# From attention to mixing: where the raw mixing weights land, and the order of the last output tiles

## The chip, the core and the metric

The kernel runs on one core of a Trainium2 chip. A core has five engines that work at the same time, each through its own queue and in program order: TensorE (PE in the profile; PEld is its weight load), VectorE (DVE), ScalarE (ACT), GpSimd (POOL) and SyncE (SP). In this kernel SP issues every DMA. An engine that waits for another one stands still with everything queued behind it. The metric is the device time of one execution in microseconds (us).

## What is computed

One block with an adaptive layer norm: attention over a sliding window of 256 keys with 32 heads, then a block that mixes neighbouring rows, then an MLP. The sequence has 2048 rows of 576 numbers, all in float32.

```python
mod = (_silu(c) @ w_mod).reshape(c.shape[0], 6, 1, -1)
sa, ca, ga, sb, cb, gb = (mod[:, i] for i in range(6))
h = _layernorm(x) * (1 + ca) + sa
x = x + ga * attention(h, wqkv, wo)          # 32 heads of 18, window 256
h = _layernorm(x) * (1 + cb) + sb
# the second block, on h:
g = _gelu(_layernorm(h) @ w1)                # four quarters of the columns,
hs = shift(g) @ w2                           # shifted by +1, -1, +2, -2 rows
x1 = h + hs
b = x1 + _gelu(_layernorm(x1) @ w3) @ w4
out = x + gb * b
```

## The kernel before

The rows are cut into 16 tiles of 128 (`t`, 0 to 15) and these into eight groups of two for the mixing. A float32 product is made of three: each operand is split into a high part (a cast to the matmul's format) and a low part (the rest), and high by high, high by low and low by high are added up. So each weight passes through ACT (the cast) and DVE or POOL (the subtraction), and each activation that PE transposed goes through ACT and DVE before the next product can use it.

Every piece of work is a small function that `at(time, function, ...)` puts into one list with a time of its own; `build` sorts the list by these times and calls the functions in that order (L1242). The times are no more than an order: they decide in which sequence each engine and SP meet their instructions. `te` is the time at which attention's two pools of buffers are closed, `T1` the time of the first mixing product, `tm(h)` the time of head h, 13 units each.

Around the change stand three streams of work.

*The end of attention.* A quad of heads u (0 to 15; four heads on two packed pairs) ends with `av` (L512, product of the exponentials P and the values V, on PE), `avs` (L529, ACT copies it from PSUM), `otr` (L533, PE transposes), `onm` (L538, DVE divides by the row sums) and `ost` (L546, SP stores it to DRAM). The last of them is u = 15.

*The output tiles.* `wotile` (L645) is the chain for one tile of rows: `orow` (SP loads the attention's rows and x), `otT` (PE transposes), `otev` (ACT and DVE split), `wom` (PE, two halves of 14 products with Wo), `woe` (DVE adds x), `ln1`, `ln1n`, `ln2`, `ln2n` (the two layer norms, on DVE, POOL and ACT) and the stores `st1`, `st2`, `st3` to three arrays in DRAM: `xp` (the residual), `hbd` (h) and `xnd` (normed h). Tiles 0 to 9 run beside the attention; tiles 10 to 15 come after `av` of u = 15, since a tile from 12 on needs its store, or stand close to it.

*The mixing.* `begin` (L706) opens the pools `mixb` and `mixa`. `w1load` and `w2load` bring the raw weights in five pieces each, `w1split` and `w2split` split them. Per group, `load` brings two rows of `xnd`, `tr` transposes, `tev` splits, `w1mm` makes five products, `w1ev` the GELU and its split, `w2mm` the second product of a tile in two halves, `w2ev` adds h (loaded by `hload`), and `st`, `nrm`, `rsum`, `xst`, `rst` make the norm and the residual for the MLP (`xpl` loads the residual; `gb` is the factor that it is scaled with, loaded at L873).

Memory sets a second order. A pool gives out buffers by tag: x1, rr, xm are three, three and two buffers of 576 floats for the mixing's residual, gf two of 256 floats for the GELU; the tag xr of `mixa` has three buffers of 640 floats, and before the change all raw W1, raw W2 and loaded rows go through these three in turn. The pools of attention and of mixing lie on the same (left) side, one over the other in time: a tile that lies over an older one waits until that one's last reader is done, tile by tile. From the bottom, attention has the four Q tiles, the three K tiles, the QS tiles, the maxima, then V, KS and P.

## Time and profile before

| | |
|---|---|
| median of 3 runs | 1869.98 us (1864.36 to 1878.24) |
| the profiled execution | 1870.27 us, span 1868.5 us |
| mean granted clock of PE | 0.971 |
| PE busy | 1731.3 us, 93% |
| DVE / POOL / ACT busy | 1094.4 / 902.3 / 707.2 us |
| DMA, mean over the span | 111 GB/s |

The page gives busy times of the engines over the span; the timeline lists instructions of an engine in order of time (start, length, engine, line, operation, tiles, count, and in brackets the idle time before it with what ended it). The windows view cuts the span into stretches: for each, its length, the busy time of PE, PEld, DVE, ACT and POOL, then the clock that was granted to PE (1.00 is full), the share of the DMA engines in use and GB/s. The waits view says who waited for whom: us in total, times, longest. Line numbers are those of the kernel before.

The change lies between 700 us and 830 us of the span: attention's last `av` starts at 719.17 us, group 0's first mixing product (L789) at 746.87 us, and group 1's at 783.30 us. From 971 us on the MLP's products (L1128 and others) fill the rest.

### The profile page before, as it was taken

The numbers are of one execution on the slowest core, as the hardware profiler recorded it, in microseconds if no ns is written. First come the engines' busy times: TensorE is split into PE (matmuls) and PEld (weight loads), VectorE is DVE, ScalarE is ACT, GpSimd is POOL, SyncE is SP. The second block draws the span as 40 slices with busy tenths as digits, with TensorE's granted clock in tenths as the row PEclk, the third lists the DMA queues.
The fourth block names the chain that finished last, engine by engine and source line by source line (L and its number), as shares of the span: only waits on it lengthen the run. The fifth ranks groups of instructions, "written<-read, shape, count | busy, mean of one in ns | idle before, by whom it ended". The sixth has DMA issues, their size and how long they took to land.

```text
span 1868.5 us, 33751 instructions
## 1 busy us (share of the span) xinstructions
PE 1731.3 (93%) x13496; PEld 1579.5 (85%) x13496; DVE 1094.4 (59%) x1801; ACT 707.2 (38%) x1210; POOL 902.3 (48%) x842
## 2 busy tenths in 40 slices
PE   6999989889999997898879999999979999999998
PEld 6788878788888986797868899999978999999997
DVE  3644244455656563566667666666676666666664
ACT  2222134344444444444433333333343333333331
POOL 3312264445454442346466655555553555555560
PEclk9999979899999998899989999999989999999999
DMA  4855552444544533565352211111224222222211
GB/s 146 312 180 180 165 152 85 118 117 133 156 134 141 149 101 113 192 216 168 115 167 68 60 55 54 55 55 56 60 71 141 60 60 60 60 60 60 59 43 51
DMA packets 156132, 206.72 MB, mean 111 GB/s; under 512 B 19012, under 2 KB 87620, under 8 KB 155400
## 3 DMA queue, kind: packets, MB, share of 16 engines
q1 hardware_dynamic: 155976, 204.57, 35.8%
q8 instruction: 106, 1.74, 0.4%
q14 instruction: 50, 0.41, 0.1%
HBM read 143.69 MB, written 60.56 MB: 109 GB/s over the span
## 4 chain that ended last, share of the span: by engine, by line
PE 45%; DVE 3%; POOL 3%; DMA 2%; ACT 1%; issue 1%; SPq 1%; POOLq 0%; DVEq 0%
PE d L1128 23%; PE pg L789 1%; PE w L838 1%; DVE W L986 1%; DMA wf<-in_B_w_dram 1%; PE u18P L1075 1%; PE u19P L1075 1%; PE u29P L1075 1%; PE u33P L1075 1%; PE u32P L1075 1%; PE u31P L1075 1%; PE u30P L1075 1%; PE u28P L1075 1%; PE u27P L1075 1%; PE u26P L1075 1%
## 5 line engine op out<-in xcount | busy, mean ns | idle before, releaser
L1128 PE MATMUL d<-W,G 128*128 128x288 f32 x3456 | 505.9, 297 | 11.9 <-DVE acc L1136 9.1
L1128 PEld LDWEIGHTS d<-W,G 128*128 128x128 f32 x3456 | 487.9, 189 | 33.6 <-DVE acc L1136 10.3
L1136 DVE TENSOR_TENSOR acc<-d,acc 128x576 f32<-128x576 f32 x288 | 216.7, 753 | 195.9 <-PE d L1128 193.9
L966 POOL TENSOR_TENSOR wf<-wf 128x384 f32<-128x384 f32 x140 | 146.6, 1068 | 337.9 <-DMA wf<-in_B_w_dram 299.8
L456 DVE TENSOR_REDUCE m<-mx 128x2 f32<-128x640 f32 x224 | 181.3, 817 | 159.5 <-PE mx L446 157.3
L504 ACT ACTIVATE P<-X 128x512 f32<-128x512 f32 (+4 forms) x320 | 180.4, 573 | 207.2 <-PE X L489 204.6
L444 PE MATMUL mx<-KD,QS 128*128 128x320 f32 (+4 forms) x512 | 157.6, 358 | 38.2 <-POOL QS L427 19.4
L427 POOL TENSOR_SCALAR QS<-QD,rowm 128x512 fp32r<-128x512 f32 x128 | 87.7, 698 | 145.4 <-DMA QD<-qd 60.7
L487 PE MATMUL X<-QD,KS 128*128 128x64 f32 (+2 forms) x704 | 151.2, 307 | 3.7 <-ACT P L504 3.3
L978 POOL TENSOR_TENSOR W<-wf,W 128x768 fp32r<-128x768 f32 x70 | 151.4, 2185 | 1.2 <-ACT W L972 1.2
L1105 DVE TENSOR_TENSOR G<-U,G 128x512 fp32r<-128x512 f32 x108 | 91.0, 843 | 100.3 <-ACT G L1098 100.3
L444 PEld LDWEIGHTS mx<-KD,QS 128*128 128x128 f32 x512 | 101.9, 199 | 45.8 <-POOL QS L427 24.2
L1096 ACT ACTIVATE U<-U 128x512 f32<-128x512 f32 x108 | 68.3, 632 | 177.6 <-DVE U L1081 177.6
L1096 ACT ACTIVATE C<-C 128x512 f32<-128x512 f32 x36 | 22.8, 632 | 280.7 <-DVE C L1081 280.7
L279 PE MATMUL qk<-hT,Wqk 128*128 128x512 f32 x504 | 121.0, 401 | 0.0
L279 PEld LDWEIGHTS qk<-hT,Wqk 128*128 128x128 f32 x504 | 95.9, 191 | 24.2 <-issue 0.9
L487 PEld LDWEIGHTS X<-QD,KS 128*128 128x128 f32 x704 | 106.7, 195 | 10.6 <-ACT P L504 7.5
L434 POOL TENSOR_SCALAR KS<-KD,rowm 128x768 fp32r<-128x768 f32 (+1 forms) x128 | 107.6, 853 | 0.0
L992 POOL TENSOR_TENSOR wf<-wf,gb 128x1152 f32<-128x1152 f32 x35 | 103.5, 2956 | 6.7 <-DMA wf<-in_B_w_dram 6.7
L446 PE MATMUL mx<-Mq,identr 128*128 128x128 f32 x448 | 101.3, 226 | 0.0
L1007 POOL TENSOR_TENSOR W<-wf,W 128x1152 fp32r<-128x1152 f32 x35 | 96.7, 2762 | 6.9 <-ACT W L1001 6.9
L972 ACT CAST W<-wf 128x1152 fp32r<-128x1152 f32 x70 | 90.3, 1319 | 21.6 <-DMA wf<-in_B_w_dram 10.8
(763 smaller groups left out, 3219.5 us busy)
## 6 DMA issues: line engine op xcount, KB each, us to landing
wf<-in_B_w_dram SPq DMA_DIRECT2D x35, 576.0 KB
wf<-in_B_w_dram SPq DMA_DIRECT2D x140, 128.0 KB
KD<-kd SPq DMA_DIRECT2D x72, 216.0 KB
QD<-qd SPq DMA_DIRECT2D x96, 144.0 KB
wf<-in_B_w_dram SPq DMA_DIRECT2D x140, 64.0 KB
qd<-qs SPq DMA_DIRECT2D x16, 512.0 KB
kd<-qs SPq DMA_DIRECT2D x16, 512.0 KB
vd<-Vst SPq DMA_DIRECT2D x16, 312.0 KB
```

Source lines behind the costliest of these rows:

```text
L279: nc.tensor.matmul(po, W[:, a, fs], H[:, c, :], start=(n == 0), stop=(n == 13))
L434: nc.gpsimd.tensor_scalar(t[:, b0:, r], src[:, b0:], M[:, 2 + r:3 + r], 0.0, op0=ALU.mult, op1=ALU.add)
L444: nc.tensor.matmul(pm[:, s, 320 - 64 * nb:320], lhs, K[:, j, 64 * (i + 5 - nb):64 * (i + 5)], start=True, stop=False)
L456: nc.vector.tensor_reduce(out=m[:, c:c + 2], in_=pm[:, :, 0:320], axis=mybir.AxisListType.X, op=ALU.max, negate=True)
L487: nc.tensor.matmul(px[:, c:c + q1 - q0], K[:, b + 4].rearrange("p r k -> p (r k)"), Q[:, j, q0:q1], start=(i == 0), stop=False)
L504: nc.scalar.activation(p[:, lo:], X["px", n, j, k][:, lo:], AF.Exp, scale=SCALE)
L966: nc.gpsimd.tensor_tensor(out=WF[:, o], in0=WF[:, a], in1=WF[:, b], op=ALU.subtract)
L978: eng.tensor_tensor(out=W[:, s0:s1, 3:5, :], in0=WF[:, 1 + s0:1 + s1, 0:2], in1=W[:, s0:s1, 0:2, :].bitcast(F32), op=ALU.subtract)
L992: nc.gpsimd.tensor_tensor(out=R4, in0=R4, in1=gb.unsqueeze(1).to_broadcast([P, 2, D]), op=ALU.mult)
L1075: nc.tensor.matmul(po, W[:, w - 1, a, :], X[:, b, :], start=(m == 0), stop=(m == 6))
L1128: nc.tensor.matmul(po, G[:, g, ta, b, ts], W[:, w, b, cs], start=(n == 0), stop=(n == 5))
L1136: nc.vector.tensor_tensor(out=a, in0=po, in1=a, op=ALU.add)
```

## The change

Six things are done at once.

- Raw W1 (five pieces), the first two row tiles of the mixing and the first piece of raw W2 get buffers of the tags x1, rr, xm and gf in `mixb`, which are asked for first in `begin` and so lie at the bottom of the left side; raw W2's last piece takes a buffer of x1. Only raw W2's pieces 1 to 3 and the rows from tile 2 on use the tag xr of `mixa`.
- Raw W1, the two row tiles and four pieces of raw W2 are loaded at `te` + 0.1 to 0.3 in place of `te` + 0.1 to 0.5 (W1), 8 and 9 (rows) and 17 to 23 (W2). The 64 last columns of the first two rows go to a buffer of their own, by two DMAs each in place of one.
- W1 is split from `te` + 0.6 on and not from 7.5, ahead of `avs` of u = 15 and of tile 10's `otT`; W2 from 8.5 and not from 19.
- The first two rows are transposed at `te` + 5.7 and 6.8, ahead of tile 10's products, and not at 15 and 16, behind tile 11's.
- `T1` is `te` + 14.3 and not `te` + 19: the mixing as a whole moves up by 4.7 units.
- The chain of u = 15 and tiles 10 to 15 are written out with times of their own (`last`). Relative to the mixing, tile 11's products stand between group 0's first products, tile 12's at their end, tiles 13 and 14 in group 1 and tile 15 in group 2. The store of u = 15 and the load of tile 12's rows stand at 13.3 and 13.4 (9.5 and 9.75 before). The load of `gb` moves from 15 to 24.

```diff
@@ attention
         for u in range(16):
             h = 2 * u + LX + 2
             at(tm(h), av, u)
+            if u == 15:
+                continue
...
+        def last(te):
+            for r in range(2):
+                at(te + 5.0 + .01 * r, avs, 15, r)
+                at(te + 9.9 + .1 * r, otr, 15, r)
+                at(te + 11.4 + .1 * r, onm, 15, r)
+            at(te + 13.3, ost, 15)
+            for t, b0, o, a, w0, w1 in ((10, 0, -8.0, 5.02, 7.9, 11.6), (11, 2, .05, 13.6, 15.95, 17.65), (12, 2, 13.4, 19.75, 21.15, 23.2),
+                                        (13, 2, 21.2, 32.1, 33.75, 35.45), (14, 2, 29.2, 37.55, 38.9, 40.6), (15, 2, 42.5, 49.85, 51.5, 53.2)):
+                at(te + o, orow, t)
+                at(te + a, otT, t, b0)
+                at(te + a + .02, otev, t)
+                for hf, w in ((0, w0), (1, w1)):
+                    at(te + w, wom, t, hf, b0)
+                    at(te + w + 2.05, woe, t, hf)
+                e = te + w1 + 2.1
+                for d, f in ((.3, ln1), (1.0, st1), (3.0, ln1n), (4.9, ln2), (5.5, st2), (7.5, ln2n), (9.5, st3)):
+                    at(e + d, f, t)
@@ mixing, begin
+            for t in range(2):
+                X["xr", t] = mb([P, D], F32, tag="x1", name=f"xmr{t}", bufs=3)
+                X["xt", t] = mb([P, 256], F32, tag="gf", name=f"xmt{t}", bufs=2)[:, 0:P]
+            X["w1", 0] = mb([P, D], F32, tag="x1", name="w1r0", bufs=3)
             X["W2"] = mb([P, 9, D], F32R, name="W2")
+            for k in range(1, 5):
+                X["w1", k] = mb([P, D], F32, tag="rr" if k < 4 else "xm", name=f"w1r{k}", bufs=3 if k < 4 else 2)
+            X["w2", 0] = mb([P, D], F32, tag="xm", name="w2r0", bufs=2)
...
@@ mixing, load
+            if t > 1:
+                X["xr", t] = ma([P, 640], F32, tag="xr", name=f"xmr{t}", bufs=3)
+                X["xt", t] = X["xr", t][:, 512:]
+            r = X["xr", t]
             nc.sync.dma_start(r[:, 0:D], self.xnd[t])
-            nc.sync.dma_start(r[:, D:], self.xnd[t][:, 512:])
+            if t > 1:
+                nc.sync.dma_start(r[:, D:], self.xnd[t][:, 512:])
+            else:
+                for u in range(2):
+                    nc.sync.dma_start(X["xt", t][:, u * TAIL:(u + 1) * TAIL], self.xnd[t][:, 512:])
@@ mixing, times
-            at(T0 + .1 + .1 * k, w1load, k)
-            at(T0 + 7.5 + 1.5 * k, w1split, k)
-            at(T0 + 17 + 2 * k, w2load, k)
-            at(T0 + 19 + 2 * k, w2split, k)
-        at(T0 + 15, lambda: nc.sync.dma_start(self.gb, self.modd[5].to_broadcast([P, D])))
+            at(T0 + .1 + .01 * k, w1load, k)
+            at(T0 + .6 + .8 * k, w1split, k)
+            at(T0 + (.2 + .01 * k if k < KC else 7.0), w2load, k)
+            at(T0 + (8.5, 11, 14.5, 17.7, 22)[k], w2split, k)
+        at(T0 + 24, lambda: nc.sync.dma_start(self.gb, self.modd[5].to_broadcast([P, D])))
@@ mix_events
-            at(s - 7, load, t)
+            at(s - 7 if t > 1 else T1 - 14.14 + .01 * t, load, t)
...
-            tile_in(i, T1 - 4 + i)
+            tile_in(i, T1 - 8.6 + 1.1 * i)
@@ build
-            T1 = te + 19.0
-            wotile(10, 33.95, 0)
-            wotile(11, 34.5, 0)
-            wotile(12, 35.22)
-            for i, d in enumerate((6.7, 18.2, 35.9)):
-                wotile(13 + i, (T1 + d - tm(0)) / HU - 0.3)
+            T1 = te + 14.3
+            last(te)
```

More of the change, by code (lines that the diff above doesn't have):

```diff
@@ L693, in attention @@
             wotile(t, 12.4 + 2 * t)
-        return tm, wotile
+        def last(te):
[15 more added lines that the diff above has]
+                    at(e + d, f, t)
+        return tm, last
     def mixing(self, T0, TB):
@@ L718, in w1load @@
         def w1load(k):
-            r = X["w1", k] = ma([P, 640], F32, tag="xr", name=f"w1r{k}", bufs=3)
+            r = X["w1", k]
             if k < KC:
@@ L740, in w2load @@
         def w2load(k):
-            r = X["w2", k] = ma([P, 640], F32, tag="xr", name=f"w2r{k}", bufs=3)
+            if k == KC:
+                X["w2", k] = mb([P, D], F32, tag="x1", name=f"w2r{k}", bufs=3)
+            elif k:
+                X["w2", k] = ma([P, 640], F32, tag="xr", name=f"w2r{k}", bufs=3)
+            r = X["w2", k]
             if k < KC:
@@ L759, in load @@
         def load(t):
-            r = X["xr", t] = ma([P, 640], F32, tag="xr", name=f"xmr{t}", bufs=3)
+            if t > 1:
+                X["xr", t] = ma([P, 640], F32, tag="xr", name=f"xmr{t}", bufs=3)
+                X["xt", t] = X["xr", t][:, 512:]
+            r = X["xr", t]
             nc.sync.dma_start(r[:, 0:D], self.xnd[t])
-            nc.sync.dma_start(r[:, D:], self.xnd[t][:, 512:])
+            if t > 1:
[3 more added lines that the diff above has]
+                    nc.sync.dma_start(X["xt", t][:, u * TAIL:(u + 1) * TAIL], self.xnd[t][:, 512:])
         def tr(t):
@@ L768, in tr @@
                 nc.tensor.transpose(pt[:, 0, k * P:(k + 1) * P], r[:, k * P:(k + 1) * P], self.ident)
-            nc.tensor.transpose(pt[:, 1, 0:P], r[:, 512:], self.ident)
+            nc.tensor.transpose(pt[:, 1, 0:P], X["xt", t], self.ident)
         def tev(t):
@@ L1224, in build @@
             t1, t2 = self.qkv(0.0, 47.0)
-            tm, wotile = self.attention(t1, t2, t1 + 6.0, HU)
+            tm, last = self.attention(t1, t2, t1 + 6.0, HU)
             te = tm(34.07)
```

## The prediction

> **What bounds the kernel now.** I read the page first: TensorE (PE) is busy 93% of the span and every other engine 59% or less, so an edit pays only where PE stands still or runs at a lower granted clock. The forecast is made against the profiled execution: 1868.5 us of span, 1870.27 us as a run, 0.3 us above the median of 1869.98 us.
>
> ```profile
> span 1868.5 us, 33751 instructions
> ...
> PE 1731.3 (93%) x13496; PEld 1579.5 (85%) x13496; DVE 1094.4 (59%) x1801; ACT 707.2 (38%) x1210; POOL 902.3 (48%) x842
> ```
>
> Next I read the timeline of PE around the place that the diff touches, from the last attention product, u = 15 at L526 (it ends at 719.17 + 4.86 = 724.03; I call this moment A), to the first product of mixing group 1 at L789 (783.30).
>
> ```profile
> 719.17 4.86 PE L526 MATMUL av<-P,V 64*32 64x320 f32 x208
> 723.96 0.66 PE L590 MATMUL pa<-ident,or 128*128 128x128 f32 x4
> ...
> 726.01 2.13 PE L611 MATMUL wo<-Wo,T 128*128 128x288 f32 x14 [1.29 <-DVE T L599]
> 727.99 1.03 PE L536 MATMUL ot<-ident,avs 128*128 128x128 f32 x8
> 728.78 2.09 PE L611 MATMUL wo<-Wo,T 128*128 128x288 f32 x14
> ...
> 740.67 0.66 PE L768 MATMUL ptm<-ident,xmr 128*128 128x128 f32 x4 [3.81 <-DMA xmr<-xnd]
> ...
> 745.89 1.12 PE L590 MATMUL pa<-ident,or 128*128 128x128 f32 x4 [2.78 <-DMA or<-od]
> ...
> 777.39 6.07 PE L838 MATMUL w<-W,Gm 128*128 128x288 f32 x28 [5.82 <-DVE xr L615]
> 783.30 1.82 PE L789 MATMUL pg<-xT,W 128*128 128x256 f32 x14
> 784.97 0.60 PE L590 MATMUL pa<-ident,or 128*128 128x128 f32 x4
> ```
>
> Brackets hold PE's idle time and what ended it: the first rows' load, the output rows' load (it follows the store of u = 15), and a long wait before the first W2 product. Then the windows view, for this stretch, the next one, and the parts at half clock (the sum line covers 741.19 to 751.43, 758.25 to 761.67 and 775.32 to 782.15).
>
> ```profile
> 724.03:783.30 59.27, 41.27 (x258) 38.77 (x259) 31.20 (x69) 21.30 (x49) 19.28 (x30) 0.83 0.60 187
> 783.30:832.47 49.17, 47.65 (x382) 47.29 (x380) 33.02 (x84) 23.57 (x54) 22.18 (x37) 1.00 0.59 197
> ...
> sum 20.49, PE 15.40 PEld 14.68 DVE 14.27 ACT 5.73 POOL 6.37; mean PE 5.13 PEld 4.89 DVE 4.76 ACT 1.91 POOL 2.12
> ```
>
> The second figure is PE's busy time: idle is 59.27 - 41.27 = 18.0 us. PE worked 15.40 us at a granted clock of 0.50, half of which, 7.7 us, a full clock would save. So the stretch loses 25.7 us, and no reordering in it can gain more. The next 49 us hold 1.5 us of idle. What is won must be won before 783.30.
>
> **Why the clock fell.** Cut into pieces of 3.41 us from a fall at 707.06, the windows view shows the fall follow an idle piece:
>
> ```profile
> 724.12:727.54 3.42, 2.13 (x16) 1.89 (x16) 0.89 (x2) 1.74 (x4) 0.00 (x0) 1.00 0.65 187
> 727.54:730.95 3.41, 3.41 (x28) 3.22 (x27) 2.26 (x7) 1.54 (x4) 1.85 (x3) 1.00 0.76 257
> ...
> 737.78:741.19 3.41, 0.52 (x5) 0.52 (x5) 0.47 (x1) 0.00 (x0) 2.15 (x3) 1.00 0.69 199
> 741.19:744.60 3.41, 1.68 (x8) 0.93 (x6) 1.92 (x5) 1.51 (x4) 0.00 (x0) 0.50 0.45 119
> ...
> 748.02:751.43 3.41, 3.41 (x18) 3.41 (x17) 0.53 (x2) 0.00 (x0) 0.14 (x1) 0.50 0.90 277
> 751.43:754.84 3.41, 2.90 (x23) 2.66 (x21) 0.00 (x0) 1.23 (x2) 0.50 (x1) 1.00 0.97 317
> ```
>
> A piece with 0.52 us of PE work is followed by half clock; one with 2.13 us is not; a full piece (3.41 us) brings full clock back.
>
> **The change part by part.**
>
> *Loads ahead of A.* SP, the queue that issues all DMAs, stands idle before A; it waited 12.6 us for the last attention product ahead of the first raw W1:
>
> ```profile
> SPq L721 <- PE av L526: 12.6, 1, 12.6
> ...
> 711.01 0.45 SPq L584 DMA_DIRECT2D xr<-in_A_x_dram  x1
> 724.12 2.05 SPq L721 DMA_DIRECT2D w1r<-in_B_w_dram  x3
> ...
> 739.46 0.43 SPq L548 DMA_DIRECT2D od<-o  x1
> 742.92 0.32 SPq L581 DMA_DIRECT2D or<-od  x1
> ```
>
> The raw W1 buffers lie over P tiles, which u = 15 reads. Now raw W1, the two first rows and the first raw W2 go to the residual's tags x1, rr, xm, gf, which open at the bottom of the same side; by the tiles' sizes (x1, gf: 8,960 bytes; W2; rr, xm: to 41,216) they lie over Q0 to Q2, K2 and QS, whose last readers are the products of heads 30 and the maxima of heads 31. So SP goes on at 711.5: row loads of tile 11 (3 DMAs), W1 (6), first rows (6, two more than before, as the 64-wide tail is now loaded twice), one W2: 16 issues. At 2.05 / 3 = 0.68 us each that is at most 10.9 us: 722.4. All of it lies beside u = 15, so it costs nothing; were the cover gone it would be 11 us of SP time ahead of everything after A (second rival). Raw W2 1 to 3 keep the old buffers: SP waits there until A, and behind it stand raw W2 4 (8 DMAs), the store of u = 15 and tile 12's rows. The store's data come only with onm, at about 735.5; the rows are issued 742.92 - 739.46 = 3.5 us later and land 745.89 - 742.92 = 3.0 us after that, near 742; PE asks for them near 747.5. Hidden, with 5 us to spare. The zero fill of gk on POOL now lies over a V tile and waits for A; only W1's POOL subtractions are queued behind it, and they are needed 11 us later. The late load of gb needs no cover until the first rsum, ten us behind it. None of this is on the path.
>
> *The order at A on ACT.* Here the change adds a wait. W1 itself still lies over V tiles that u = 15 reads, so its casts can start between 719.3 (if nothing held them) and 724.1 (A); V is read to the end but for the last blocks of keys, so I take 723.4. They stand ahead of avs and of tile 10's otev in ACT's queue, where before otev came first (724.65).
>
> ```profile
> 724.65 0.58 ACT L597 CAST T<-pa 128x512 fp32r<-128x512 f32 x1 [4.78 <-PE pa L590]
> ...
> 725.29 1.10 ACT L531 COPY avs<-av 128x512 f32<-128x512 f32 x2
> 727.55 0.62 ACT L733 CAST W<-w1r 128x512 fp32r<-128x512 f32 x1 [1.17 <-DMA w1r<-in_B_w_dram]
> ...
> 728.28 0.62 ACT L733 CAST W<-w1r 128x512 fp32r<-128x512 f32 x1
> ...
> 725.27 0.69 DVE L599 TENSOR_TENSOR T<-pa,T 128x512 fp32r<-128x512 f32 x1 [15.62 <-ACT T L597]
> ```
>
> Five pairs of casts at 728.28 - 727.55 = 0.73 us: 727.05. Two avs, 1.10: 728.15. L597, 0.58: 728.7. L599, 0.69: 729.4, and tile 10's product starts 0.05 us later, as it did at 726.01. PE meanwhile has tile 10's transposes (to 724.6) and the two first rows', now moved here: ten transposes, about 1.0 us by the pace of L536 (eight in 0.79). It is done at 725.7 and idles **3.7 us** where it idled 1.29.
>
> *The clock.* From A on PE works some 1.5 us in the piece 724.12 to 727.54: between 0.52 (fell) and 2.13 (did not). If it falls at 727.54, the next piece, busy from 729.4, is not full, and half clock lasts to 734.36: 4.9 us, 2.5 lost. If it falls at 730.95 it lasts to 734.36: 1.7 lost. I take **2.1**; bounds 0 and, by the longest spell shown (741.19 to 751.43), 5.1. [...]
>
> *From there to group 1.* The work of PE is the same; one thing is moved out of the stretch, tile 13 (a row of transposes as at 784.97, and two L611 products), which goes behind 783.30's product and costs the same there. So the new loss is only waits. Walking PE's queue from 729.4: tiles 10 to 12 (six products at 727.99 - 726.01 = 1.98: 11.9), eight transposes 0.8, two otT at 0.45, five W1 products at 784.97 - 783.30 = 1.67, two rows' transposes 1.0, and 2.1 of slow clock bring it to the first W2 product near 754.5. That product needs woe of tile 12, behind which DVE's queue is full: the tail of W2's split, ln1n of tile 11, w1ev, tev, woe.
>
> ```profile
> 735.42 1.75 DVE L624 SCALAR_TENSOR_TENSOR h<-xr,b10mv,cb 128x576 f32<-128x576 f32 x1
> ...
> 773.34 0.76 DVE L756 SCALAR_TENSOR_TENSOR w2r<-W,w2r 128x576 f32<-128x576 f32 x1 [4.75 <-DMA hbd<-h]
> ...
> 774.86 0.42 DVE L803 TENSOR_TENSOR Gm<-gf,Gm 128x256 fp32r<-128x256 f32 x1
> 775.20 0.69 DVE L777 TENSOR_TENSOR xT<-ptm,xT 128x512 fp32r<-128x512 f32 x1
> ...
> 776.79 0.45 DVE L615 TENSOR_TENSOR xr<-wo,xr 128x288 f32<-128x288 f32 x1
> 777.16 0.81 DVE L624 SCALAR_TENSOR_TENSOR h<-xr,b12mv,cb 128x576 f32<-128x576 f32 x1
> ...
> 778.81 0.45 DVE L615 TENSOR_TENSOR xr<-wo,xr 128x288 f32<-128x288 f32 x1
> 779.18 0.45 DVE L117 BATCH_NORM_STATS2 c12st<-h 128x6 f32<-128x288 f32 x1
> ...
> 780.15 0.41 DVE L117 BATCH_NORM_STATS2 b13st<-xr 128x6 f32<-128x288 f32 x1
> ```
>
> W2's tail (774.86 - 773.34 = 1.52) can start when ACT has cast it, near 751.1 by my walk of ACT's queue; then ln1n 1.65 (778.81 - 777.16), w1ev 0.34, tev 0.8 (half of 776.79 - 775.20) and woe 0.45: 755.9, so PE waits **1.4 us**. The second half waits for the next woe, behind tev 0.8, ln2's statistics 0.97 (780.15 - 779.18) and itself 0.45, against the 1.98 of the first half: **0.3 us**. Tile 13's transposes, now behind group 1's first product, need the bank of the second w2ev, behind 0.97, 1.65, 0.45, 0.97 and 0.45 on DVE, 4.5 us, against 4.0 on PE: **0.5 us**. L624 took 1.75 us at 735.42 and 0.81 at 777.16; two such slow passes in this chain, **1.9 us**. Bounds for these four together: 0 (DVE ahead of PE) and 6 us (as the wait of 5.82 today). Behind that the 1.5 us of idle in the next 49 us say that PE covers the rest.
>
> **The sum.** New loss: 3.7 + 2.1 + 1.4 + 0.3 + 0.5 + 1.9 = 9.9 us; old loss 25.7; gain 15.8 us. 1870.27 - 15.8 = **1854.5 us**, 0.8% less. The lines beyond 783.30 keep their order relative to the mixing groups, so I carry the gain to the end unchanged.
>
> **Rivals.** *One, more than 1%.* ACT's casts start under u = 15 (719.3), tile 10's product starts near 727, the clock stays up. Loss: 1.3 (as at 726.01) and 4.1 of DVE's waits, 5.4; gain 20.3, **1850 us**. For it: ACT is idle then and raw W1 may have landed. Against it: W1's place over V.
>
> *Two, the loads do not come earlier*, because the new buffers are also let go only at A. Then SP issues 16 DMAs from 724.1 on; first rows come after tile 11's and W1's nine (6.1 us) and their own six (4.1 us) and land 3.0 us later, 737; PE's queue has them ahead of tile 10's product, which starts at 738 and not 729.4, 8.6 us worse: 1854.5 + 8.6 = **1863 us**. Against it: those tiles' readers end before heads 31.
>
> *Three, slower: the clock.* The gap at A tips the clock at a place where no full piece follows, and it stays at half. Each us so spent loses a half; the gain of 15.8 is eaten when 32 us more of PE time, as long as the walk from 729.4 to group 1 and some way into it, run so; at 36 us it is 1854.5 + 18 = **1872 us**. Against it: the longest spell in these rows held 7.2 us of PE work. [...]
>
> **How the numbers follow.** The forecast's case (losses of 7 to 15 us) has a chance of 0.58, rival one 0.30, rival two 0.08, rival three 0.04. The runs of the kernel before spread over 1864 to 1878, so 1% (18.7 us) is about what a measurement tells from no change. Range 1845 to 1863: it holds the first two cases with that spread. Faster by over 1%: rival one's greater part and the forecast's lower edge, 0.36. Slower by over 1%: 0.03. Within: 0.61.
>
> **What would show it.** Right: SP issues W1's loads near 713; L733 begins 723 to 724; L611 of tile 10 begins near 729.4, with 3 to 4 us idle before it named to DVE T; half clock for at most 5 us behind it; the first W2 product near 756; group 1's first product near 760 to 761. Wrong: L733 before 722 (rival one), L721 at 724 (two), half clock past 740 (three), or idle time in groups 1 to 3 that the row of 783.30 to 832.47 does not have.

## The result, and the profile after

| | before | after |
|---|---|---|
| median of 7 runs each | 1871.78 us (1864.36 to 1878.24) | **1853.64 us** (1847.43 to 1860.52) |
| ratio, 95% interval | | 0.9899 (0.9879 to 0.9919) |
| the profiled execution | 1870.27 us, span 1868.5 us | 1853.12 us, span 1851.3 us |

The forecast was 1854.5 us. Two lines of the page of after: PE's share is the same, and the span is 17.2 us shorter.

```profile
span 1851.3 us, 33769 instructions
...
PE 1725.0 (93%) x13496; PEld 1572.3 (85%) x13496; DVE 1093.2 (59%) x1801; ACT 706.9 (38%) x1210; POOL 903.9 (49%) x842
```

PE's timeline of after, from the last attention product on (line numbers are now those of the kernel after: W1 products at L828, W2 at L877, ACT's W1 casts at L761):

```profile
716.85 4.68 PE L526 MATMUL av<-P,V 64*32 64x320 f32 x187
722.88 0.53 PE L526 MATMUL av<-P,V 64*32 64x128 f32 x21 [1.36 <-issue]
...
727.36 2.74 PE L611 MATMUL wo<-Wo,T 128*128 128x288 f32 x14 [2.16 <-DVE T L599]
...
752.98 4.11 PE L877 MATMUL w<-W,Gm 128*128 128x288 f32 x28 [1.21 <-DVE xr L615]
...
756.93 1.82 PE L828 MATMUL pg<-xT,W 128*128 128x256 f32 x14
...
760.04 0.33 PE L592 MATMUL pb<-ident,or 128*128 128x128 f32 x1 [0.63 <-DVE x L881]
...
776.48 2.13 PE L877 MATMUL w<-W,Gm 128*128 128x288 f32 x14 [0.31 <-DVE xr L615]
779.64 5.81 PE L877 MATMUL w<-W,Gm 128*128 128x288 f32 x42 [1.04 <-DVE xr L615]
...
804.47 3.94 PE L877 MATMUL w<-W,Gm 128*128 128x288 f32 x28 [1.59 <-DVE x L881]
```

Two readings. The waits for the first rows and the output rows (3.81 and 2.78 us before) are gone, and 5.82 us ahead of the first W2 product have become 1.21. New is the bracket of the second row: the last attention product, one unbroken block of 208 matmuls before, stops behind matmul 187 for 1.36 us, and the profile names nothing that it waited for ("issue").

I call the start of that product S (719.17 before, 716.85 after) and compare times from S. The 2.3 us between the two arise ahead of the change and say nothing about it: in the profiles of seven kernels whose work up to there is the same (after, e5, e6, e7, e9, e10, e12) S lies anywhere from 715.62 to 721.86. The windows view of after, for PE alone (length, PE's busy time, clock, DMA share, GB/s), for the product, the stretch to group 1's first product (756.93), groups 1 and 2, groups 3 to 4, and from there to the MLP's second waiting product (972.20, the first of its products that waits for the sums `acc`):

```profile
716.85:723.41 6.56, 5.20 (x211) 1.00 0.88 223
723.41:756.93 33.52, 30.14 (x226) 0.95 0.60 183
756.93:785.28 28.35, 26.36 (x204) 1.00 0.63 212
785.28:808.25 22.97, 21.38 (x171) 1.00 0.55 185
808.25:849.81 41.56, 38.36 (x307) 1.00 0.58 189
849.81:972.20 122.39, 96.96 (x644) 0.97 0.44 142
```

The same points, read from PE's rows and counted from S, show where the time came from:

| us after S | group 1 | group 2 | group 3 | group 4 | group 5 | MLP's second waiting product |
|---|---|---|---|---|---|---|
| before | 64.13 | 85.23 | 106.37 | 126.36 | 152.83 | 274.85 |
| after | 40.08 | 68.43 | 91.40 | 108.95 | 132.96 | 255.35 |
| gain | 24.05 | 16.80 | 14.97 | 17.41 | 19.87 | 19.50 |

At group 1, about 4.3 us of the 24.05 are only tile 13's work (its transposes and two products, by the pace of PE's rows), which now stands behind that point; so the lead there is 19.75 us. It falls to 14.97 at group 3 and comes back to 19.5. In the span the account closes: 2.3 us ahead of S, 19.5 from there, and 4.6 us lost behind 972, together 17.2. Those 4.6 lie in MLP code that the change does not touch, and they are no more than its spread: from that product to the end the fourteen profiles took 873.2 to 880.1 us (before 874.5, after 879.1).

### The profile page after: what moved, and what is told of

Read it like the earlier page. It is cut to its first block, busy times and chain, and to the rows that moved or that the text cites. A ratio compares the mean times of both kernels' runs of the same rounds, so it can differ in the third digit from the quotient of the medians.

```text
span 1851.3 us, 33769 instructions
## 1 busy us (share of the span) xinstructions
PE 1725.0 (93%) x13496; PEld 1572.3 (85%) x13496; DVE 1093.2 (59%) x1801; ACT 706.9 (38%) x1210; POOL 903.9 (49%) x842
## 4 chain that ended last, share of the span: by engine, by line
PE 74%; DVE 7%; DMA 6%; POOL 5%; issue 3%; ACT 3%; SPq 2%; POOLq 0%; DVEq 0%; ACTq 0%
PE d L1167 23%; PE qk L279 6%; PE av L526 4%; PE v L309 3%; PE mx L444 3%; PE wo L611 3%; PE pg L828 3%; PE X L487 3%; DMA QD<-qd 2%; PE w L877 2%; DVE m L456 1%; PE X L489 1%; PE pm L177 1%; PE ot L536 1%; DVE W L1025 1%
## 5 line engine op out<-in xcount | busy, mean ns | idle before, releaser
L1144 DVE TENSOR_TENSOR G<-U,G 128x512 fp32r<-128x512 f32 x108 | 95.3, 882 | 99.8 <-ACT G L1137 99.8
```

## The experiments

All ratios are against the kernel before, run on the same chip. Times "from S" are of the profiled execution, one per kernel. e5, e6, e9, e10 and e11 were run once each (1856.71, 1863.35, 1858.80, 1849.20 and 1862.26 us), for their profile only. Ahead of the experiments stood this theory: the loads that come earlier, through the new buffers, carry the gain, and the order alone would meet their wait. Its rival: the order does most of it.

**The buffers and early loads alone, in the old order** (e1). Some of the lines:

```diff
-            if u == 15:
-                continue
...
-            at(T0 + .6 + .8 * k, w1split, k)
+            at(T0 + 7.5 + 1.5 * k, w1split, k)
...
-            T1 = te + 14.3
-            last(te)
+            T1 = te + 19.0
+            wotile(10, 33.95, 0)
...
```

> The new buffers and the early loads, with the order of before for everything else (T1 = te + 19, splits and tiles 10 to 15 as before). Measured from the start of the last attention product to the first product of mixing group 5, the kernel before took 152.8 us and the changed one 133.0. Theory one, the waits that went were waits for loads, so the buffers carry the gain: 133 to 137 us, and a time 16 to 20 us under the kernel before. Theory two, the gain needs the new order (T1 earlier, W1 split at once): 143 us or more, and a gain of 10 us or less.

1855.23 us (1851.04 to 1858.26), ratio 0.9909 (0.9888 to 0.9930). Group 1 begins 45.50 us after S with tile 13 done, so 41.2 by the count of after. PE's timeline and the windows view from the product's end to group 1:

```profile
727.14 0.53 PE L526 MATMUL av<-P,V 64*32 64x128 f32 x21 [0.94 <-issue]
729.65 2.14 PE L611 MATMUL wo<-Wo,T 128*128 128x288 f32 x14 [1.29 <-DVE T L599]
...
763.14 4.05 PE L875 MATMUL w<-W,Gm 128*128 128x288 f32 x28 [0.90 <-DVE xr L615]
```

```profile
727.67:767.02 39.35, 33.99 (x258) 1.00 0.63 193
```

In the old order tile 10's product waits 1.29 us for T (its transposed rows), as in the kernel before, the clock stays up, and the waits of this stretch add up to 39.35 - 33.99 = 5.4 us. Group 5 begins at S + 134.04, within the first theory's 133 to 137. The loads alone bring nearly all of the gain, and what the new order adds to them (0.9899 against 0.9909) is less than the runs can resolve. The lead is also kept in the old order: 18.63 us at group 1, 18.60, 18.61, 18.74 and 18.79 at groups 2 to 5, and 17.50 at the MLP's product, where the changed kernel's goes down to 14.97 and up again.

**The new order alone, with the old buffers** (e2): the raw weights and the first rows go through the three buffers of tag xr again, which the last product releases.

```diff
-                X["xr", t] = mb([P, D], F32, tag="x1", name=f"xmr{t}", bufs=3)
...
-            r = X["w1", k]
+            r = X["w1", k] = ma([P, 640], F32, tag="xr", name=f"w1r{k}", bufs=3)
```

> The new order with the old buffers: raw W1, raw W2 and the first rows again go in turn through the three buffers that wait for the last attention product. Theory one (buffers carry the gain): SP issues the first raw W1 only at the end of that product, the first rows come 12 us later, and PE waits for them ahead of tile 10's product; the same stretch takes 145 us or more and the gain over the kernel before is under 8 us, or none. Theory two (order carries it): 138 us or less and a gain of 12 us or more.

1866.07 us (1860.95 to 1871.90), ratio 0.9964 (0.9946 to 0.9982): 6.0 us under the 1872.06 of before, a third of what the whole change brings. PE stands with the transposes of the first rows, now moved ahead of tile 10's products, and waits for their load:

```profile
719.71 4.86 PE L526 MATMUL av<-P,V 64*32 64x320 f32 x208
736.53 1.12 PE L790 MATMUL ptm<-ident,xmr 128*128 128x128 f32 x4 [11.27 <-DMA xmr<-xnd]
```

Group 1 comes at S + 48.84, 8.76 us later than in after, and group 5 at S + 143.02, where the first theory expected 145 or more and the second 138 or less. Half clock lasts from 728.4 to 741.9 us, across that wait and behind it (the four transposes take 1.12 us, as against 0.60 at 760.31 us). So the order without the loads waits, and the loads without the order do not wait here. And the product of 208 matmuls has no gap here: it appears only where loads run beside it (DMA share of the product 0.51 to 0.96 in the twelve profiles with a gap, 0.01 in before).

**Fewer transfers beside the last product** (e3): the tail columns are copied by DVE, and the raw W2 piece whose buffer is free early is asked for behind the others.

```diff
-                for u in range(2):
-                    nc.sync.dma_start(X["xt", t][:, u * TAIL:(u + 1) * TAIL], self.xnd[t][:, 512:])
+                nc.vector.tensor_copy(X["xt", t].rearrange("p (u f) -> p u f", u=2), r[:, 512:].unsqueeze(1).to_broadcast([P, 2, TAIL]))
...
-            at(T0 + (.2 + .01 * k if k < KC else 7.0), w2load, k)
+            at(T0 + (.2 + .01 * (k or KC) if k < KC else 7.0), w2load, k)
```

> The changed kernel with less DMA traffic during the last attention product: the tail columns of the first rows are copied by DVE in place of four small DMAs, and the first piece of raw W2 is issued behind pieces 1 to 3, so after that product. In the changed kernel the product shows a gap of 1.36 us that waits for nothing the profile shows, while the DMA engines are 86% busy and one packet of PE's instructions is among their load; before, with idle DMA engines, the same packet came and no gap. Theory one, the instructions queue behind the data: no gap over 0.3 us, the product takes 4.8 to 5.2 us and not 6.6, and the stretch to group 5 is 1 to 2 us shorter. Theory two, the gap is chance or something else: it is there as before.

The gap shrinks to 0.20 us, with the DMA share of that product at 0.61 and not 0.88. But the next wait grows to 4.04 us. PE's timeline, then DVE's:

```profile
722.35 0.52 PE L526 MATMUL av<-P,V 64*32 64x128 f32 x21 [0.20 <-issue]
...
728.70 3.07 PE L611 MATMUL wo<-Wo,T 128*128 128x288 f32 x14 [4.04 <-DVE T L599]
```

```profile
723.49 1.79 DVE L764 TENSOR_TENSOR W<-w1r,W 128x512 fp32r<-128x512 f32 x1 [1.04 <-PE pa L590]
...
725.74 1.77 DVE L764 TENSOR_TENSOR W<-w1r,W 128x512 fp32r<-128x512 f32 x1
```

The wait grows by 1.88 us for two reasons. PE comes 1.16 us sooner to a T that the gap did not hold up. And T itself is later: DVE's two W1 subtractions took 1.79 and 1.77 us here, in after 0.69 and 1.55, and T stands behind them in DVE's queue. POOL starts its own subtractions only when the product has ended; without the gap that is 1.16 us sooner (5.97 and 7.13 us after S), and so both of DVE's run beside them, as in after only the second did. Tile 10's product starts at S + 11.23, in after at S + 10.51, and group 5 at S + 135.92, 3 us later than in after, where 1 to 2 us sooner was expected. 1855.86 us, ratio 0.9912 (0.9882 to 0.9942): no gain over after.

**Another order on ACT** (e4): the first avs and tile 10's split stand ahead of the last two W1 casts.

```diff
-                at(te + 5.0 + .01 * r, avs, 15, r)
+                at(te + 3.0 + .2 * r, avs, 15, r)
...
-            for t, b0, o, a, w0, w1 in ((10, 0, -8.0, 5.02, 7.9, 11.6), (11, 2, .05, 13.6, 15.95, 17.65), (12, 2, 13.4, 19.75, 21.15, 23.2),
+            for t, b0, o, a, w0, w1 in ((10, 0, -8.0, 3.1, 7.9, 11.6), (11, 2, .05, 13.6, 15.95, 17.65), (12, 2, 13.4, 19.75, 21.15, 23.2),
...
-            at(T0 + .6 + .8 * k, w1split, k)
+            at(T0 + (.6, 1.4, 2.2, 3.4, 4.2)[k], w1split, k)
```

> The changed kernel with ACT's order at the end of attention altered: pieces 0 to 2 of W1 are cast first, then the first avs, tile 10's otev, the second avs, and only then pieces 3 and 4. Theory one (the 2.2 us gap ahead of tile 10's product comes from the casts that stand ahead of its otev, and it is this gap that lets the clock fall): the gap is under 0.5 us, no stretch of half clock follows within 10 us, and group 1's first product stands 2.5 to 4 us earlier after the start of the last attention product than in the changed kernel (40.1 us there). Theory two (the clock falls because of the attention product and the transposes, whatever ACT does): the gap goes but the half clock stays, and 1 to 2 us are gained. In time: 2 to 4 us under the changed kernel, about 0.2%, which five rounds can hardly tell.

```profile
723.30 0.52 PE L526 MATMUL av<-P,V 64*32 64x128 f32 x21 [1.02 <-issue]
...
726.20 2.12 PE L611 MATMUL wo<-Wo,T 128*128 128x288 f32 x14 [0.58 <-DVE T L599]
```

The wait for T is 0.58 us (under 0.5 was expected), the clock stays up (1.00 from 717.1 to 759.85 us), and group 1 comes at S + 37.31, 2.77 us earlier than in after: so the casts ahead of T make that wait. The MLP's second waiting product comes at S + 256.31, 1 us later than in after; where the 2.8 us go is taken up with e12. The time is 1851.97 us (1848.99 to 1854.74), ratio 0.9893 (0.9872 to 0.9914), which cannot be told from after; nor can a gain of 2.8 us be excluded by it.

**Work in the gap ahead of tile 10's product** (e5 and e6): 14 products, or 19 transposes, behind the first rows' transposes, to see whether the gap is what brings the clock down.

```diff
+            o = X["pt", 1][:, 1, 128:416]
+            for _ in range(14):
+                nc.tensor.matmul(o, self.identr, self.Mk.rearrange("p a b -> p (a b)")[:, 0:288], start=True, stop=True)
...
+        at(T1 - 7.2, self.fill)
```

In e6 the two lines of the loop are these:

```diff
+            for _ in range(19):
+                nc.tensor.transpose(o, X["xr", 1][:, 0:P], self.ident)
```

> The changed kernel with 14 products of 288 columns, whose results nobody reads, put into the gap ahead of tile 10's output product (added work; the output is the same). Theory one (the clock fell after 727.4 because TensorE had done next to nothing for more than two microseconds): the products fill 1.9 to 2.5 us of the gap, the granted clock stays at 1.00 in the 7 us behind it, the first 28 products of L611 take 2.1 us instead of 2.74, and group 1 begins 38.0 to 38.9 us after the start of the last attention product instead of 40.08. Rival (the clock falls for another reason, a draw of the run or the long load before it): half clock for some 3.4 us all the same, L611 at 2.5 us or more, group 1 at 39.7 us or later.

> The same gap filled with 19 transposes of 128 columns instead of products (added work; the output is the same). [...] If transposes count like products: the clock stays at 1.00, and group 1 begins at 38.0 to 38.9 us, as expected of the run with products.

Both miss their purpose: the added work shares a bank with a tile that DVE has yet to read, so it waited for DVE and stood behind the gap. The rows of the two kernels:

```profile
728.49 3.60 PE L813 MATMUL ptm<-Mk,identr 128*128 128x288 f32 x14 [2.88 <-DVE xT L824]
```

```profile
732.51 3.69 PE L813 MATMUL ptm<-ident,xmr 128*128 128x128 f32 x19 [3.92 <-DVE xT L824]
```

Behind gaps of 2.88 and 3.92 us both ran at half clock (granted 0.50 from 729.07 to 730.78 us in e5 and from 732.49 to 734.20 in e6). On what fills a gap they say nothing.

**The same work placed where it waits for nothing** (e9, e10): put into the list ahead of the reads of that bank.

```diff
-        at(T1 - 7.2, self.fill)
+        at(T1 - 7.25, self.fill)
```

> The 14 products of the earlier run, now put where they wait for nothing: behind the transposes, ahead of the reads of their bank (added work; the output is the same). Theory one (the clock falls because TensorE stands idle for 1.8 us or more in one piece): the products begin within 0.3 us of the last transpose, take 1.8 to 2.1 us, the idle piece ahead of tile 10's product is under 1 us, and the granted clock stays at 1.00 in the 7 us behind it, as long as the gap inside the attention product is under 1.6 us. Rival (the clock falls for another reason): half clock for some 3.4 us behind the products all the same.

> The same with 19 transposes in place of the products (added work; the output is the same). [...] If transposes count like products: the clock stays at 1.00, as in the run with products.

With products, then with transposes:

```profile
727.71 2.09 PE L813 MATMUL ptm<-Mk,identr 128*128 128x288 f32 x14
730.18 2.14 PE L611 MATMUL wo<-Wo,T 128*128 128x288 f32 x14 [0.38 <-DVE T L599]
```

```profile
724.21 2.24 PE L813 MATMUL ptm<-ident,xmr 128*128 128x128 f32 x19
726.20 2.11 PE L611 MATMUL wo<-Wo,T 128*128 128x288 f32 x14
```

The clock stays at 1.00 in both (14 products of L611 in 2.14 and 2.11 us, against 2.74 in after), and group 1 comes at S + 38.50 and 38.53 instead of 40.08. Tile 10's product itself starts no sooner than in after (S + 10.52 and 10.58, against 10.51), so what is won is the clock. In these profiles, one for each kernel, it fell with the idle piece and stayed up without it, and transposes kept it up as products did.

**The last of these, timed** (e12, the same kernel as e10).

> The changed kernel with the 19 transposes in the gap, as in the run before, now timed (added work; the output is the same). Theory one (the 1.6 us by which group 1 comes earlier than in the changed kernel is kept to the end): 1850.5 to 1852.5 us, and the MLP's second waiting product 253 to 254.5 us after the start of the last attention product. Rival (a lead of one or two microseconds is given back behind group 3, to waits for VectorE and GpSimd): 1852.6 to 1855.5 us, not to be told from the changed kernel, with that product at 255 us or later.

1855.49 us (1851.40 to 1858.71), ratio 0.9905 (0.9890 to 0.9920). Group 1 comes at S + 39.09, 0.99 us sooner than in after, and the MLP's product at S + 257.05, 1.7 us later. By these figures it is the rival, but not by its reason. The lead is still 1.02 us at group 3 and 0.66 at group 4, and goes within group 4. There PE stands ahead of the transposes of new rows. The timeline puts it down to "issue" in e12 and to ACT in after, but DVE's last read of the transposes before them (L1113, in after L1105) ends at 840.63 + 0.29 = 840.92, 0.11 us ahead of PE's start, and in after at 839.91, also 0.11 ahead; so I read it as a wait for that bank, by these times alone. PE in after and in e12:

```profile
840.02 0.63 PE L807 MATMUL ptm<-ident,xmr 128*128 128x128 f32 x4 [1.72 <-ACT Gm L841]
```

```profile
841.03 0.63 PE L807 MATMUL ptm<-ident,xmr 128*128 128x128 f32 x4 [2.58 <-issue]
```

and the pass of DVE that makes the difference, in after and in e12:

```profile
838.75 0.43 DVE L842 TENSOR_TENSOR Gm<-gf,Gm 128x256 fp32r<-128x256 f32 x1
...
839.62 0.29 DVE L1105 TENSOR_TENSOR A<-pt,A 64x128 fp32r<-64x128 f32 x1
```

```profile
839.19 0.99 DVE L849 TENSOR_TENSOR Gm<-gf,Gm 128x256 fp32r<-128x256 f32 x1
...
840.63 0.29 DVE L1113 TENSOR_TENSOR A<-pt,A 64x128 fp32r<-64x128 f32 x1
```

The same pass takes 0.43 us in one profile and 0.99 in the other. But it is after's profile that stands apart, not e12's: a wait of 2.55 to 2.59 us stands at this place in that of before and in eleven of the twelve experiments' (2.12 in e7), and after alone has 1.72. Behind the wait the clock then goes one way or the other. In eight of those twelve profiles (before, e1, e5, e6, e9 to e12) half clock follows for some 3.4 us, and from group 4 to group 5 they took 26.3 to 26.5 us; in the other four (e2, e3, e4, e8) the clock stays at 1.00, and they took 24.8 to 25.0. After took 24.01. In e12 the clock falls within the piece shown:

```profile
841.03:844.45 3.42, 3.42 (x21) 0.70 0.24 92
```

So e12's lead is lost to a shorter wait and a better clock in the one profile of after, neither of which the six profiles in the same order (e5, e6, e9 to e12) show. That a lead of this size is given back is therefore not shown. e4 loses 0.83 us in group 4, to the longer wait alone, and 2.2 more from group 5 to the MLP's product, a stretch in whose code the kernels do not differ and which took from 121.2 to 124.8 us in the fourteen profiles. Leads of 1 to 3 us are below what one profile of each kernel, or these runs' times, can follow to the end.

**Tile 13 ahead of the first W2 product again** (e7): are three output tiles in groups 1 and 2 one too many for DVE?

```diff
-                                        (13, 2, 21.2, 32.1, 33.75, 35.45), (14, 2, 29.2, 37.55, 38.9, 40.6), (15, 2, 42.5, 49.85, 51.5, 53.2)):
+                                        (13, 2, 16.5, 25.4, 26.4, 27.9), (14, 2, 29.2, 37.55, 38.9, 40.6), (15, 2, 42.5, 49.85, 51.5, 53.2)):
```

> The changed kernel with the transposes and the output product of tile 13 ahead of the first W2 product, as before the change, so that only two output tiles lie in groups 1 and 2. Theory one (three output tiles in group 1 load VectorE so that its sums come late: 0.31 and 1.04 us of waits for xr and 1.59 for x that were not forecast): group 1 begins 44.0 to 45.0 us after the start of the last attention product, group 2 at 66.8 to 67.6 instead of 68.43, the MLP's second waiting product 1.0 to 1.6 us earlier than 255.35, and the time is 1852.0 to 1852.8. Rival (tile 13 waits at its new place for what it waited for at the old one, or the waits are the groups' own): group 2 at 68.1 us or later, time 1853.3 to 1855.

```profile
756.40 0.65 PE L590 MATMUL pa<-ident,or 128*128 128x128 f32 x4 [1.11 <-DVE xr L615]
758.49 0.33 PE L592 MATMUL pb<-ident,or 128*128 128x128 f32 x1 [1.43 <-DVE xr L615]
```

Tile 13 waits at its new place for the sums of tile 12, 2.5 us in two pieces, half clock follows these (from 759.9 us, for 3.4 us), and group 2 comes at S + 69.36 (after: 68.43), as the rival expected: the tile waits for DVE's sums wherever it stands. 1856.01 us (1849.37 to 1859.11), ratio 0.9907 (0.9882 to 0.9932), above both expected ranges and not to be told from after.

**ACT's order and fewer transfers together** (e8), the tail columns now copied by POOL, not DVE. To the edit of e4 come:

```diff
+                nc.gpsimd.tensor_copy(X["xt", t].rearrange("p (u f) -> p u f", u=2), r[:, 512:].unsqueeze(1).to_broadcast([P, 2, TAIL]))
...
+            at(T0 + (.2 + .01 * (k or KC) if k < KC else 7.0), w2load, k)
```

> The changed kernel with ScalarE's order of the earlier run (the first half of the attention output copied ahead of the last two W1 casts), the tail columns copied by GpSimd in place of four small transfers, and the first raw W2 piece asked for behind the others. Theory one (the gap inside the last attention product goes with the transfers, the wait for T goes with ScalarE's order, and both gains add): no gap over 0.3 us in that product, a wait for T of 0.6 us or less, no half clock behind it, group 1 at 36.0 to 37.0 us from the product's start, and 1850.0 to 1851.5 us. Rival (the lead is given back behind group 3, to waits for other engines that do not come earlier): group 1 as early, but the MLP's second waiting product at 255 us or later, and 1851.7 to 1853.5 us.

```profile
721.19 0.53 PE L526 MATMUL av<-P,V 64*32 64x128 f32 x21 [0.26 <-issue]
...
725.17 2.14 PE L611 MATMUL wo<-Wo,T 128*128 128x288 f32 x14 [1.59 <-DVE T L599]
```

The gap is nearly gone, and the wait for T is back at 1.59 us, so the two gains do not add: T comes when ACT and DVE have made it (product at S + 8.92, in e4 at S + 8.60), however soon PE asks. Group 1 comes at S + 37.39, the MLP's product at S + 255.15, and the time is 1853.72 us (1849.96 to 1857.62), ratio 0.9900 (0.9874 to 0.9926). The lead at group 1 is again not seen at the MLP's product, with the reservation made for e12. No timed variant that keeps the early loads can be told from after.

**What the gap in the product is** (e11): 40 short products, whose results nobody reads, go into PE's instructions long before.

```diff
+            for _ in range(40 if (t, hf) == (9, 0) else 0):
+                nc.tensor.matmul(po[:, 0:64], self.identr, self.Mk.rearrange("p a b -> p (a b)")[:, 0:64], start=True, stop=True)
```

> The changed kernel with 40 short products, whose results nobody reads, added to TensorE's instructions in tile 9's output product, long before the last attention product (added work; the output is the same). Theory one (the gap inside that product is TensorE waiting for its next instructions, which come by the same DMA engines as the raw weights): the gap moves by 40 instructions, from behind 187 of the 208 matmuls to behind some 147, and is 0.9 to 2.5 us long. Rival (the gap waits for data, or belongs to the products behind it): it stays behind matmul 187.

```profile
722.71 3.98 PE L526 MATMUL av<-P,V 64*32 64x320 f32 x147
729.60 1.45 PE L526 MATMUL av<-P,V 64*32 64x320 f32 x61 [2.91 <-issue]
```

The gap moves by exactly 40, from behind matmul 187 to behind matmul 147. It belongs to a place in the stream of instructions and not to any data. The same profile shows what ACT's W1 casts wait for:

```profile
730.81 0.62 ACT L763 CAST W<-w1r 128x512 fp32r<-128x512 f32 x1 [7.40 <-PE av L526]
```

They start 8.10 us after S here, with the gap ahead of them, and 4.59 or 4.60 us after S in after and in the nine experiments that keep its order and loads and have the gap, if any, behind matmul 187.

## Why the prediction was right, and where it was not

*The mechanism was right.* The loads ahead of the product carry the gain: e1 alone makes 1855.23 us, e2 alone 1866.07. SP issued W1 at 710.68 us, 6.17 us ahead of S, just as far as the forecast's 713 lies ahead of 719.17, so rival two (loads not earlier) is out. The half clock behind the gap ended after 3.4 us, so rival three (stuck at half) is out too.

*"All of it lies beside u = 15, so it costs nothing"* was wrong for the product itself, which took 723.41 - 716.85 = 6.56 us, not 4.86. The 1.7 us are 1.36 of gap and 0.34 behind it. The forecast looked at SP's time and at the buffers, not at what else the DMA engines do: one packet on an instruction queue, which I take for PE's, goes over them during this product, in before too, where they are idle (share 0.01) and no gap is seen. But the 1.7 us were not lost on top, since they came off the next wait.

*The gap ahead of tile 10's product*: 3.7 us forecast, 2.16 measured. The chain that makes it came out as worked out. Counted from S, the forecast let ACT's casts start at 723.4 - 719.17 = 4.23 us and tile 10's product at 10.23; measured are 4.59 and 10.51:

```profile
721.44 0.62 ACT L761 CAST W<-w1r 128x512 fp32r<-128x512 f32 x1 [3.89 <-DMA xmt<-xnd]
...
725.04 1.05 ACT L531 COPY avs<-av 128x512 f32<-128x512 f32 x2
```

PE was 1.8 us later than forecast at this wait, nearly all of it from the gap inside the product, and so waited that much less. Together the two pieces are 2.16 + 1.70 = 3.86 us, against 3.7. The time 721.44 looks like the sign for rival one (casts before 722), but that sign was set on the times of before, where 722 is 2.83 us after S; the casts started 1.8 us later than that. Rival one (casts early, tile 10's product 7.8 us after S, the clock up) did not come. The profile of after names a DMA as what the first cast waited for; eight of the experiments' profiles with the same start name the last product, and e11, where the cast moves with the gap, bears out the forecast's reason: W1 lies over V, which the product reads almost to its end.

*The clock*: forecast 2.1 us lost, measured 1.7: half clock for some 3.4 us in one piece, from about 728.5 us (the window shown begins a little ahead of it). The windows view:

```profile
728.36:731.78 3.42, 3.42 (x18) 0.54 0.30 75
```

The earlier of the forecast's two falls, at 727.54, did not come: counted from S it stands at 8.37 us, and the granted clock of after is 1.00 up to 11.51 us (728.36). Nor did the clock fall behind transposes alone in e10 and e12. In e12's timeline PE did nothing but transposes from 723.54 us until the wait that ended at 728.77, and worked at full clock behind it (granted 1.00 from 721 to 737 us):

```profile
723.54 0.66 PE L590 MATMUL pa<-ident,or 128*128 128x128 f32 x4
...
725.23 2.24 PE L813 MATMUL ptm<-ident,xmr 128*128 128x128 f32 x19
728.77 2.13 PE L611 MATMUL wo<-Wo,T 128*128 128x288 f32 x14 [1.30 <-DVE T L599]
```

Had transposes not counted as work for the clock, that would have been 5.2 us without work, longer than any gap here that the clock survived (2.91 us). The forecast's own reading, that the clock falls behind a piece with 0.52 us of PE work and not behind one with 2.13, does not hold as a rule even in the profile of before: by the same view its piece from 703.65 to 707.06 us has 2.32 us of work, and half clock follows.

*DVE's waits up to group 1*: 1.4 us forecast, 1.21 measured; 0.3 against none; 0.5 against 0.63. The 1.9 us for two slow DVE passes did not show as idle time of PE in the stretch: idle there is 33.52 - 30.14 = 3.38 us, which is 2.16 + 1.21. Together the new loss was 3.86 + 1.7 + 1.21 = 6.8 us up to group 1, and 0.63 behind it. The forecast had 9.9 in all; the slow passes are the term that was most off. The difference of 3.1 us is most of the 4.0 by which the lead at group 1 was larger than the forecast's gain.

*"PE covers the rest"*, that is, no further waits in groups 1 and 2: wrong. With tile 13's 0.63, waits of 0.31, 1.04 and 1.59 us for DVE's sums are new there: 3.6 of the 4.8 us by which the lead shrinks to group 3; the rest I can't place. They come with the new order of the output tiles: e1, in the old order, lost nothing there. Before, these groups ran without a pause, as the windows view of before shows (in the first two rows length and busy time are equal):

```profile
783.30:804.40 21.10, 21.10 (x171) 1.00 0.59 196
804.40:825.54 21.14, 21.14 (x171) 1.00 0.55 187
825.54:845.53 19.99, 17.84 (x141) 1.00 0.60 196
845.53:872.00 26.47, 22.25 (x170) 0.94 0.49 159
```

*"I carry the gain to the end unchanged"* held only on balance. The lead was 19.75 us at group 1 (15.8 forecast), 14.97 at group 3, and 19.5 at the MLP, since the waits that before had in groups 3 and 4 (the last two rows: 19.99 - 17.84 = 2.15 us of idle, then 4.22 and a lower clock) were shorter in the profile of after. Of the 4.9 us that came back, 2.4 arose in group 3, which took 17.5 to 18.4 us in every profile with the new order and 19.9 to 20.0 in the two with the old (before, e1). The other 2.5 arose in group 4 and are luck of this profile: the six of the same order (e5, e6, e9 to e12) took 26.3 to 26.4 us there, about as before did. The wait that after has at 1.72 us is this one in before:

```profile
860.61 1.06 PE L768 MATMUL ptm<-ident,xmr 128*128 128x128 f32 x4 [2.56 <-issue]
```

So the number came out within a microsecond of the median by errors that cancelled, and by luck: the forecast's gain was 15.8 us and the measured one, median to median, 18.1, but the forecast counted from 1870.27 us, and the median of before is 1871.78. In the span: 15.8 us forecast, 4.0 more at group 1, 4.8 lost by group 3, 4.5 back by the MLP, 4.6 lost in it, 2.3 won ahead of S: 17.2. The last two are the spread of code that is the same in both kernels.

## What to carry to other kernels

A transfer put beside PE's work is not free merely because PE needs none of its data: look at what else uses the DMA engines in that time. Then look at what PE waits for next: here the 1.4 us stop came off the wait behind it, and taking it away (e3) won nothing. When several things are changed at once, measure the parts: here the loads alone gave nearly all of the gain and kept their lead through the groups, while the new order won 1.1 us more at group 1 and lost 4.8 in the next two groups, mostly to waits for DVE. A lead of one to three microseconds, as in e4, e8 and e12, has to be followed through more than one profile of the kernel that it is compared with, since a single wait behind it is followed by half clock or not (eight of twelve were here). When the casts that release a stage can overlap the work before it, find which instruction frees their buffer: here it was one shortly ahead of the product's end, 4.59 us after its start.

## What the hardware showed unexpectedly

*PE seems to wait for its own instructions when the DMA engines are busy.* The gap, in the profiles that have it at matmul 187 or 147: none where the loads come behind the product (before, DMA share 0.01, and e2); 0.20 and 0.26 us in e3 and e8, where the traffic ended early; 0.75 to 2.91 us in the other nine runs and in after. In seven of them (after, e5, e6, e7, e9, e10, e12) all that comes before that place is the same, and the gap ranged from 0.75 to 2.45 us. The traces tell more. During each of these products one packet starts on the instruction queue that I take for PE's (106 packets of 16 KB in the span), 1.93 and 1.98 us after S in before and e2, and 2.31 to 4.82 us after S where loads run beside it. In all twelve profiles with a gap, PE goes on 2.31 to 2.59 us after the start of that packet, however long the gap is:

| | before | e2 | e3 | e8 | e12 | e1 | e4 | after | e9 | e6 | e7 | e10 | e5 | e11 |
|---|---|---|---|---|---|---|---|---|---|---|---|---|---|---|
| packet starts, us after S | 1.93 | 1.98 | 2.31 | 2.45 | 2.91 | 3.23 | 3.27 | 3.52 | 3.57 | 3.53 | 3.94 | 4.04 | 4.82 | 4.38 |
| gap, us | none | none | 0.20 | 0.26 | 0.75 | 0.94 | 1.02 | 1.36 | 1.30 | 1.42 | 1.85 | 1.76 | 2.45 | 2.91 |
| PE goes on, us after the packet's start | | | 2.57 | 2.49 | 2.52 | 2.39 | 2.43 | 2.51 | 2.41 | 2.57 | 2.59 | 2.40 | 2.31 | 2.51 |

So the later the packet, the longer the gap. In before and e2 the same distance would let PE go on some 4.4 us after S, ahead of the end of matmul 187 at 4.68, and there is no gap. That the packet holds PE's next instructions is argued from this and from the shift by 40; no run changed that queue alone. If the packet is what PE waits for, its cost was hidden with the DMA engines idle (share 0.01 in before, no gap) and not with them 0.88 busy, as in after (1.36 us).

*The length of a gap alone does not decide on the clock.* At the end of attention half clock followed gaps of 1.85 us (e7, inside the product), 2.16 (after), 2.88 (e5), 3.92 (e6) and 4.04 (e3 and e11); none followed 1.59 (e8), 1.76 (e10, inside the product), 2.45 (e5) and 2.91 (e11, both inside the product). e7's second spell, at tile 13's new place, followed two waits of only 1.11 and 1.43 us. Of the twelve waits of 2.55 to 2.59 us in group 4, eight were followed by half clock and four were not. Each of these spells lasted about 3.4 us, but for the one behind e11's 4.04 us, which lasted twice that; the rows of before (741.19 to 751.43 us, 10.24 us) and e2 (728.4 to 741.9, 13.5 us) show spells of three and four times that length around longer waits. What else decides between half and full clock behind the same gap, no run here shows.
